# Twenty low-part subtractions move from GpSimd to VectorE, and all units get a new order

## The chip, the cores and the metric

The kernel runs on one core of a Trainium2 chip. The metric is the device time of one execution in microseconds, and less is better. TensorE (PE) multiplies, VectorE (DVE) and ScalarE (ACT) do elementwise work, GpSimd (POOL) does a little of it and issues some transfers, and SyncE (SP) issues the other transfers.

## The reference

Pooled attention is followed by a gated feed-forward layer:

```python
k_p = k.reshape(B, H, Sp, 8, D).mean(axis=3)       # B = H = 8, S = 576, D = 64, Sp = 72
v_p = v.reshape(B, H, Sp, 8, D).mean(axis=3)
scores = matmul(q, k_p.T) / sqrt(D)
attn = exp(scores - max); attn = attn / (attn.sum() + 1e-9)
x = matmul(attn, v_p)        # then heads side by side: 4608 tokens x 512
out = (1 / (1 + exp(-(x @ w_gate))) * (x @ w_val)) @ w_out     # 512 -> 1536 -> 512
```

## The kernel before

The 4608 tokens are worked on in nine blocks of 512. Block 0 goes through attention and the whole layer in a first pass (`first_pass`), in which the 64-bit weights also arrive, are turned into float32 (`conv`, `oconv`) and are split into a high and a low part; attention of blocks 1 and 2 lies in that pass too. Blocks 1 to 8 follow in four pairs. Each pair is one multiplication by Strassen's scheme with seven products: first the two products with the weights of gate and value (`product`; its banks in PSUM are the tiles `chain`), then the one with the output weights (`second_sums`; tiles `acc`). Attention of the next blocks is woven between.

Every operand x is a high part (x rounded to the format fp32r, by ACT) and a low part (x minus the high part, by DVE or POOL), and each product takes three matmuls: high by high, high by low, low by high. So a tile such as `hs` (hidden values), `xo` (tokens), `parts` and `oparts` (weights), `ph` and `pl` (attention weights), `vh` and `vl` (values) is made by one ACT copy and one subtraction.

The values: `vsum` adds eight rows, `vhi` (ACT) writes `vh`, `vlo` writes `vl`; `rsum`, `rhi` and `rlo` do the same for the last eight keys of four heads (tile `other` or `vrc`), and `vput` (POOL) places those in `vres`. In blocks 3 to 8 DVE makes every `vl`. In the first pass, for blocks 1 and 2, POOL does (`v_lo`, `r_lo`).

In blocks 5 to 8 the attention weights are not turned by PE. DVE turns them in blocks of 32 (`turned`, tile `turn`), POOL sends each tile to memory in 4, 8 or 12 small transfers, and a further POOL transfer brings it back (`pt`, `pr`). The tile `turn` has one buffer, so the next turning waits until all of those transfers have read it.

The weights' parts are kept in memory (`kept...`) and loaded again for each pair by transfers on SP's queue.

No scheduler decides the order. The code first records every unit (one instruction, or a group that stays together). The string `LATER` is a list of unit numbers, worked out by a planner beforehand, and the units are issued in that order. Each engine runs its own instructions strictly in that order, and so do the queues of SP and POOL; an instruction that waits holds up everything behind it on its engine.

```python
for n in LATER.split() or range(len(book.units)):
    for taken in book.units[int(n)]:
        taken.issue(link)
```

Of the kernel before, what the change touches and what calls it, by code (L numbers as in the profile page):

```python
# [11 lines left out]
F32 = mybir.dt.float32  # L12
# [314 lines left out]
def attention_then_ffn(ctx: ExitStack, tc: tile.TileContext, qT, kT, vm, vr, vn, sums8, wgv, wo, const, out, outT):  # L327
# [800 lines left out]
    def first_pass():  # L1128
# [202 lines left out]
        def v_lo(j, p):  # L1331
            i = slot(j, p)
            if j:
                for r in (slice(0, D), slice(D, P)):
                    nc.gpsimd.tensor_tensor(out=vl[i][r, r], in0=vs[j, p][r], in1=vh[i][r, r].bitcast(F32), op=ALU.subtract)
                return
# [196 lines left out]
```

## Time and profile before

| What | Value |
| --- | --- |
| Median of 3 runs | 926.18 us |
| Lowest and highest of them | 920.35 and 928.2 us |
| The profiled execution's own time | 930.2 us |
| Its span, first to last instruction | 928.1 us |
| Mean granted clock of TensorE | 0.996 |

The profile shows one execution. Its span leaves out 2.1 us of its time. PE, DVE, ACT, POOL are the engines; PEld is the loading of weights into PE; SPq is SP's queue. All of the recorded instructions carry line L314, because a helper issues them, so the rows are told apart by the tiles that they write and read.

### The profile page before, as it was taken

Reading aid. Unit: us, or ns where it says so; the run is one execution under the profiler, and the core shown is the slowest. Engines: PE = TensorE matmul, PEld = TensorE weight load, DVE = VectorE, ACT = ScalarE, POOL = GpSimd, SP = SyncE. Lnnn points to the kernel's source line nnn. Section 1 sums busy time; section 2 is a strip of 40 time slices with the busy share of each in tenths; the row PEclk is TensorE's granted clock in tenths of the full one; section 3 lists DMA queues with packets and bytes.
Section 4 is the critical chain, followed back from the end, with each engine's and each line's share of the span. In section 5 each row is a group of like instructions: output and inputs, shape, how many; then the busy total and the mean of one; then the engine's idle time right before and its main releaser. Section 6 shows DMA issues by size and latency. Waiting matters only on the chain.

```text
span 928.1 us, 12622 instructions
## 1 busy us (share of the span) xinstructions
PE 901.8 (97%) x4188; PEld 739.7 (80%) x4188; DVE 653.0 (70%) x1024; ACT 550.7 (59%) x1136; POOL 170.8 (18%) x328
## 2 busy tenths in 40 slices
PE   6999998999999998999999999999999999999997
PEld 5778777888888876887888888888888788888886
DVE  7988786998888988755668987444579572332863
ACT  7999895888878654643546664535255553224352
POOL 1122202011121004435244204042212100000000
PEclk9999999999999999999999999999999999999999
DMA  9897897698878688786887797767647857465653
GB/s 348 286 333 299 308 331 288 222 354 303 295 253 284 224 270 257 250 300 204 293 282 225 238 323 215 275 215 257 213 145 246 282 176 255 160 207 189 215 182 114
DMA packets 98448, 234.67 MB, mean 253 GB/s; under 512 B 13008, under 2 KB 33872, under 8 KB 96848
## 3 DMA queue, kind: packets, MB, share of 16 engines
q1 hardware_dynamic: 85328, 203.97, 65.4%
q0 software_dynamic: 13056, 29.90, 9.4%
q8 instruction: 33, 0.54, 0.2%
q14 instruction: 31, 0.25, 0.1%
HBM read 174.58 MB, written 59.24 MB: 252 GB/s over the span
## 4 chain that ended last, share of the span: by engine, by line
PE 75%; DMA 7%; DVE 7%; ACT 6%; issue 3%; POOL 2%; SPq 0%; DVEq 0%; ACTq 0%; POOLq 0%
PE chain L314 46%; PE acc L314 22%; PE sc L314 3%; PE av L314 3%; DMA turned<-turn 2%; DMA h<-keptwG 1%; DMA oparts<-keptS 1%; DVE early L314 1%; DMA keptwV<-w 1%; DMA oparts<-keptO 1%; ACT early L314 1%; POOL turned L314 1%; DVE hs L314 1%; DVE w L314 1%; DMA raw<-in_vr 1%
## 5 line engine op out<-in xcount | busy, mean ns | idle before, releaser
L314 PE MATMUL chain<-xo,parts 128*128 128x512 f32 x2316 | 543.8, 392 | 2.4 <-ACT chain L314 0.9
L314 PEld LDWEIGHTS chain<-xo,parts 128*128 128x128 f32 x2316 | 431.4, 188 | 96.2 <-DVE parts L314 2.2
L314 PE MATMUL acc<-hs,oparts 128*128 128x512 f32 x1008 | 238.1, 392 | 5.3 <-DVE hs L314 3.7
L314 PEld LDWEIGHTS acc<-hs,oparts 128*128 128x128 f32 x1008 | 188.2, 188 | 47.3 <-DVE hs L314 4.9
L314 POOL DMA_DIRECT2D turned<-turn x192 | 105.2, 550 | 254.9 <-DVE turn L314 211.0
L314 DVE TENSOR_TENSOR y<-chain,sV 128x512 f32<-128x512 f32 x46 | 31.3, 685 | 80.6 <-PE chain L314 62.7
L314 DVE TENSOR_TENSOR hs<-h,hs 128x1024 fp32r<-128x1024 f32 x52 | 62.9, 1216 | 16.0 <-ACT hs L314 16.0
L314 ACT CAST hs<-h 128x1024 fp32r<-128x1024 f32 x52 | 54.4, 1050 | 25.6 <-PE acc L314 23.2
L314 ACT COPY chain<-chain 128x512 f32<-128x512 f32 x46 | 26.6, 577 | 70.0 <-PE chain L314 66.0
L314 ACT COPY sV<-chain 128x512 f32<-128x512 f32 x46 | 26.7, 584 | 47.8 <-PE chain L314 38.5
L314 ACT CAST hs<-s 128x1024 fp32r<-128x1024 f32 x36 | 37.6, 1051 | 25.3 <-DVE s L314 18.1
L314 ACT ACT_TABLE_LOAD x39 | 50.0, 1283 | 1.5 <-DVE pm L314 0.9
L314 DVE TENSOR_TENSOR hs<-s,hs 128x1024 fp32r<-128x1024 f32 x36 | 43.4, 1217 | 9.0 <-ACT hs L314 8.9
L314 DVE TENSOR_TENSOR y<-chain,sG 128x512 f32<-128x512 f32 x46 | 30.9, 683 | 24.5 <-PE chain L314 11.8
L314 DVE TENSOR_TENSOR h<-chain,gate 128x512 f32<-128x512 f32 x46 | 31.3, 682 | 22.0 <-PE chain L314 18.0
L314 ACT COPY sG<-chain 128x512 f32<-128x512 f32 x46 | 26.8, 589 | 30.2 <-PE chain L314 30.1
L314 ACT ACTIVATE gate<-chain 128x512 f32<-128x512 f32 x46 | 26.9, 597 | 29.0 <-PE chain L314 28.4
L314 PE MATMUL sc<-kbd,raw 128*128 128x144 f32 (+1 forms) x262 | 41.9, 298 | 2.2 <-POOL kbd L314 2.0
L314 PEld LDWEIGHTS sc<-kbd,raw 128*128 128x128 f32 (+1 forms) x262 | 33.4, 176 | 11.5 <-issue 3.4
L314 PE MATMUL acc<-oparts,hs 128*128 128x512 f32 x144 | 40.0, 407 | 0.0
L314 DVE TENSOR_REDUCE m<-sc 128x4 f32<-128x288 f32 x48 | 21.6, 451 | 17.5 <-PE sc L314 17.5
L314 ACT ACTIVATE gate<-y 128x512 f32<-128x512 f32 x46 | 28.5, 631 | 5.6 <-DVE y L314 5.5
(195 smaller groups left out, 1119.3 us busy)
## 6 DMA issues: line engine op xcount, KB each, us to landing
oparts<-keptS SPq DMA_DIRECT2D x48, 512.0 KB, 4.7
oparts<-keptO SPq DMA_DIRECT2D x72, 256.0 KB, 4.4
raw<-in_wgv SPq DMA_DIRECT2D x12, 1024.0 KB, 8.3
out<-o SPq DMA_DIRECT2D x34, 256.0 KB, 4.4
raw<-in_kT SPq DMA_DIRECT2D x28, 288.0 KB, 4.7
raw<-in_qT SPq DMA_DIRECT2D x29, 256.0 KB, 4.9
raw_o<-in_wo SPq DMA_DIRECT2D x12, 512.0 KB, 6.4
raw<-in_vm SPq DMA_DIRECT2D x24, 256.0 KB, 5.2
```

The source lines that it names most:

```text
L314: return self._book.take(lambda: f(*args, **named))
```

## The change

Two subtractions change their engine, and the order of all units is another. The units themselves, their number and what they compute stay as they were. In the first pass 16 instructions that write `vl` (four heads' pairs, two blocks, two halves) and 4 that write the low part of the last keys leave POOL for DVE.

```diff
 LATER = """
-5 4 3 6 10 2 7 13 24 17 20 12 8 27 26 16 18 30 9 0 21 22 34 19 35 36 25 42 49 50 39 38 83 32 31 11 41 43 47 73 29 55
...
-                    nc.gpsimd.tensor_tensor(out=vl[i][r, r], in0=vs[j, p][r], in1=vh[i][r, r].bitcast(F32), op=ALU.subtract)
+                    nc.vector.tensor_tensor(out=vl[i][r, r], in0=vs[j, p][r], in1=vh[i][r, r].bitcast(F32), op=ALU.subtract)
...
-            nc.gpsimd.tensor_tensor(
+            nc.vector.tensor_tensor(
                 out=vrc[j, g][64:96], in0=vsr[j, g][64:96], in1=vrc[j, g][64:96].bitcast(F32), op=ALU.subtract
             )
```

Three places show what the order does. The first is late in the first pass, on the engine that makes `vl4_103`, the low part of a pair of heads of block 2; before, this is POOL:

```order
L314 TENSOR_TENSOR vl1_100<-early_216,vh1_95 64x64 x2
L314 TENSOR_TENSOR vl4_103<-early_216,vh4_98 64x64
L314 TENSOR_TENSOR vl0_99<-early_216,vh0_94 64x64
L314 TENSOR_SCALAR vres4_108<-other_221,cst_84 96x64 x2
L314 TENSOR_SCALAR vres0_104<-other_221,cst_84 96x64
L314 TENSOR_SCALAR vres1_105<-other_221,cst_84 96x64
...
L314 TENSOR_TENSOR vl4_103<-early_216,vh4_98 64x64
L314 TENSOR_TENSOR vl0_99<-early_216,vh0_94 64x64
```

In the change it is DVE, and the rows around it are conversions of weights (`w4`, `parts`, `w_o`):

```order
L314 TENSOR_TENSOR vl4_103<-early_216,vh4_98 64x64
L314 SCALAR_TENSOR_TENSOR w4_392<-w4_392,raw64_380 128x1024
L314 TENSOR_TENSOR early4_217<-tp_393,early4_217 128x512
L314 TENSOR_TENSOR r3_389<-rest_388,r3_389 128x4x32
L314 TENSOR_TENSOR parts_402<-w4_392,parts_402 128x2x256
L314 TENSOR_TENSOR parts_405<-w4_392,parts_405 128x2x256
L314 TENSOR_TENSOR vl4_103<-early_216,vh4_98 64x64
L314 TENSOR_SCALAR w_o_400<-w_o_400 128x1024
```

The second half of `vl4_103` stood behind six placings of `vres` on POOL, and now stands behind five DVE instructions after its first half, among the conversions.

The second place is on PE at the same stage, where the first `acc` matmul needs `oparts_406` from ACT. Before:

```order
L314 MATMUL chain_401<-xo1_266,parts_397 128x512 x6
L314 MATMUL chain_401<-xo2_271,parts_397 128x512 x6
L314 MATMUL chain_398<-xo1_266,parts_395 128x512 x6
L314 MATMUL chain_410<-xo1_266,parts_405 128x512 x6
L314 MATMUL chain_410<-xo2_271,parts_405 128x512 x6
L314 MATMUL chain_398<-xo2_271,parts_395 128x512 x6
L314 MATMUL acc_315<-oparts_406,hs_404 128x512
```

The same place in the change:

```order
L314 MATMUL chain_398<-xo1_266,parts_395 128x512 x6
L314 MATMUL chain_398<-xo2_271,parts_395 128x512 x6
L314 MATMUL chain_401<-xo1_266,parts_397 128x512 x6
L314 MATMUL chain_401<-xo2_271,parts_397 128x512 x6
L314 MATMUL chain_410<-xo1_266,parts_405 128x512 x6
L314 MATMUL chain_407<-xo1_266,parts_402 128x512 x6
L314 MATMUL chain_407<-xo2_271,parts_402 128x512 x6
L314 MATMUL chain_410<-xo2_271,parts_405 128x512 x6
L314 MATMUL acc_313<-oparts_406,hs_404 128x512
```

The twelve matmuls of `chain_407` now stand ahead of the first `acc` matmul; before, they stood behind it.

The third place is on DVE at the end of the first pair, between the turning of the rest (`turn_848`) and the next turning of block 5 (`turn_855`); `hs_809` and `hs_813` are low parts that `acc` matmuls need soon. Before:

```order
L314 STREAM_TRANSPOSE turn_848<-r3_846 128x384
...
L314 TENSOR_TENSOR o_811<-acc_756,sV5_774 128x512
L314 TENSOR_TENSOR hs_809<-h_423,hs_809 128x1024
L314 TENSOR_TENSOR s_783<-s_783,xs0_495 128x1024
L314 STREAM_TRANSPOSE turn_855<-pm_853 128x512
L314 TENSOR_TENSOR pm_866<-e_819,rz_843 128x512
L314 TENSOR_TENSOR hs_813<-h_424,hs_813 128x1024
L314 TENSOR_TENSOR xo6_796<-s_783,xo6_796 128x1024
L314 TENSOR_TENSOR s_783<-xs0_495,s_783 128x1024
```

The same place in the change:

```order
L314 STREAM_TRANSPOSE turn_848<-r3_846 128x384
...
L314 TENSOR_TENSOR xo6_796<-s_783,xo6_796 128x1024
...
L314 TENSOR_TENSOR hs_807<-h_425,hs_807 128x1024
L314 TENSOR_REDUCE ks_883<-raw_884 128x72
L314 TENSOR_TENSOR hs_809<-h_423,hs_809 128x1024
L314 TENSOR_TENSOR hs_813<-h_424,hs_813 128x1024
L314 TENSOR_TENSOR s_783<-xs0_495,s_783 128x1024
L314 STREAM_TRANSPOSE turn_855<-pm_853 128x512
L314 TENSOR_TENSOR vl0_99<-vs_859,vh0_94 64x64
```

`hs_813`, `xo6_796` and the last sum `s_783` stood behind the turning, and now stand ahead of it.

## Rows read from the trace of the kernel before

**Rows 1.** The page's part 1: busy time, share of the span, instructions of each engine.

```profile
PE 901.8 (97%) x4188; PEld 739.7 (80%) x4188; DVE 653.0 (70%) x1024; ACT 550.7 (59%) x1136; POOL 170.8 (18%) x328
```

**Rows 2.** Busy time by stretch: engines in us, granted clock, DMA share, GB/s.

```profile
20.00:140.00 120.00, 115.24 (x559) 91.66 (x559) 103.45 (x164) 114.00 (x263) 21.49 (x40) 1.00 0.90 315
140.00:160.00 20.00, 17.21 (x85) 14.36 (x84) 12.44 (x20) 11.38 (x28) 6.62 (x12) 0.93 0.83 299
360.00:380.00 20.00, 16.31 (x67) 12.70 (x66) 13.41 (x16) 10.63 (x18) 7.84 (x15) 0.91 0.68 215
760.00:860.00 100.00, 100.00 (x443) 82.75 (x442) 29.69 (x46) 32.25 (x56) 0.00 (x0) 1.00 0.62 205
```

**Rows 3.** PE's waits: total us, times, longest; the whole span.

```profile
PE sc L314 <- DMA h<-in_qT: 5.5, 1, 5.5
PE acc L314 <- DVE hs L314: 3.7, 1, 3.7
PE av L314 <- POOL vl L314: 2.8, 1, 2.8
PE sc L314 <- POOL kbd L314: 2.0, 2, 1.6
...
PE acc L314 <- DMA oparts<-keptS: 1.0, 2, 0.7
PE chain L314 <- ACT chain L314: 0.9, 1, 0.9
...
PE chain L314 <- DVE y L314: 0.5, 1, 0.5
```

**Rows 4.** The timeline near 153 us: start, us, engine, operation, idle before.

```profile
152.38 2.50 POOL L314 TENSOR_SCALAR vres<-other,cst 96x64 fp32r<-96x64 f32 x6
...
154.87 2.48 DVE L314 TENSOR_TENSOR xo<-xs,xo 128x1024 fp32r<-128x1024 f32 x2
154.97 2.55 POOL L314 TENSOR_TENSOR vl<-early,vh 64x64 fp32r<-64x64 f32 x2
...
156.32 0.45 PE L314 MATMUL av<-ph,vl 128*128 128x384 f32 x1 [2.79 <-POOL vl L314]
```

**Rows 5.** The timeline from 352 to 371 us.

```profile
352.50 4.91 POOL L314 DMA_DIRECT2D turned<-turn  x9 [55.75 <-DVE turn L314]
...
358.09 1.62 POOL L314 DMA_DIRECT2D turned<-turn  x3 [0.68 <-DMA turned<-turn]
...
365.98 0.71 DVE L314 STREAM_TRANSPOSE turn<-pm 128x512 f32<-128x512 f32 x1 [4.22 <-DMA turned<-turn]
...
367.34 1.22 DVE L314 TENSOR_TENSOR hs<-h,hs 128x1024 fp32r<-128x1024 f32 x1
...
368.61 2.36 PE L314 MATMUL acc<-hs,oparts 128*128 128x512 f32 x5 [3.69 <-DVE hs L314]
```

**Rows 6.** The timeline from 417 to 425 us.

```profile
417.09 0.71 DVE L314 STREAM_TRANSPOSE turn<-pm 128x512 f32<-128x512 f32 x1 [2.76 <-issue]
...
421.65 1.66 PE L314 MATMUL chain<-xo,parts 128*128 128x512 f32 x6 [0.46 <-DVE y L314]
...
424.20 2.13 PE L314 MATMUL chain<-xo,parts 128*128 128x512 f32 x8 [0.89 <-ACT chain L314]
```

**Rows 7.** The tile `vl`: count, ns min/median/max, first and last start.

```profile
L314 DVE TENSOR_TENSOR vl<-vs,vh x40: 152/220/224, 195.2 to 689.4; 64x64 fp32r<-64x64 f32 x40
L314 POOL TENSOR_TENSOR vl<-early,vh x16: 309/342/1307, 62.0 to 156.3; 64x64 fp32r<-64x64 f32 x16
```

**Rows 8.** Groups by form: count, busy us, mean ns, idle before and its releasers.

```profile
L314 POOL TENSOR_TENSOR other<-early,other 32x64 fp32r<-32x64 f32 x4 | 1.3, 315 | 9.0 <-ACT other L314 9.0
L314 DVE STREAM_TRANSPOSE turn<-pm 128x512 f32<-128x512 f32 x16 | 11.3, 706 | 16.0 <-DMA turned<-turn 13.2 <-issue 2.8
```

**Rows 9.** Transfers: count, KB each, median us from issue to landing.

```profile
oparts<-keptS SPq DMA_DIRECT2D x48, 512.0 KB, 4.7
...
parts<-keptG0C SPq DMA_DIRECT2D x3, 512.0 KB, 6.8
```

307 rows, old and new, of the table LATER are left out of this document.

## The prediction

> **What bounds the kernel now.** I read the engines' busy time first. PE is busy 901.8 of 928.1 us, 97% [rows 1]; the other engines are not the bound on average. The change takes no matmul away, so it can only give back time in which PE waits or runs at the lower clock. The idle part is 928.1 − 901.8 = 26.3 us. The mean granted clock of 0.996 costs about 0.004 × 928.1 = 3.7 us more. Together that is 30.0 us, and no order of the same units can win more than that.
>
> The stretches come second, because the mean hides where these 30 us lie. Late in the program, from 760 to 860 us, PE is busy 100.00 of 100.00 us at full clock: 443 matmuls, 226 ns each [rows 2]. Nothing is to be had there. From 20 to 140 us it is busy 115.24 of 120.00, so 4.76 us are lost, and here ACT is busy 114.00 and DVE 103.45 of 120: ACT is the tight engine, DVE has 16.55 us left. Two stretches show a clock under 1: 0.93 from 140 to 160 and 0.91 from 360 to 380, each beside a long idle time of PE.
>
> The waits come third; they name what PE waited for [rows 3]. The longest, 5.5 us for the first transfer, is the start and stays. Then 3.7 us for `hs`, 2.8 us for `vl` from POOL, 2.0 us for `kbd` from POOL, 1.0 us for loads of `oparts`, and small ones for ACT's `chain` (0.9) and DVE's `y` (0.5).
>
> The timelines tell where the two long ones come from. Near 153 us POOL is still at six `vres` until 154.9 us and only then makes two `vl`, in 2.55 us, while DVE runs two 128x1024 subtractions; PE's `av` starts after 2.79 us of idle [rows 4]. Near 353 us the turning of the rest is sent to memory in 12 transfers, which POOL issues from 352.5 to 359.7 us. The next turning on DVE has no other buffer, waits 4.22 us for them and starts at 365.98. The low part `hs` stands behind it and starts at 367.34, and PE gets its operand at 368.61, after 3.69 us [rows 5].
>
> **The change part by part.** The sum is made against the profiled execution's 930.2 us.
>
> *Low parts on DVE.* Sixteen `vl` at DVE's 220 ns instead of POOL's 342 [rows 7], and four of the last keys (32x64; POOL takes 315 ns [rows 8]; no DVE row has this shape, so I take the 220 ns too): 20 × 0.22 = 4.4 us more on DVE. POOL loses at least 16 × 0.342 + 1.3 = 6.8 us. All of it lies before 160 us. If DVE bound PE there, the 4.4 us would come on the path; with 16.55 us of DVE idle and ACT as the tight engine I take them as covered. If that cover is gone, they cost up to 4.4.
>
> The trace shows that two of these on POOL took 2.55 us beside DVE's two-input subtractions, and the slowest 1307 ns against 309 at best [rows 4, 7]. The Trainium skill, "SBUF — State Buffer", section "SBUF: two separate sides", says that DVE and GpSimd share a port pair as an exclusive lock, and the loser is held up entirely; the trace agrees with its 1307 ns. By the rule the move also ends a mutual hold-up of about 1 us a piece at most, which the sum has as part of the 153 us term.
>
> *The order up to 140 us.* Twelve matmuls of `chain_407` now stand ahead of the first `acc` matmul that needs `oparts_406` from ACT. That gives ACT 12 × 0.226 = 2.7 us more to make it. Of the 4.76 us that PE loses in this stretch I take 2.0 back. Bounds: −2.7 (all of the slack counts) and +4.4 (DVE, above).
>
> *The stall at 153 us.* In the change the two halves of `vl4_103` stand five DVE instructions apart, instead of behind six `vres`. The wait of 2.79 us goes, and with it the lower clock that followed: 0.07 × 20 = 1.4 us. That is −4.2. Bounds: −4.2 and 0, since an instruction of the 128x1024 kind in front takes DVE 1.24 us each [rows 4], and PE may wait for that in place of POOL. I take the whole because the order now puts the last half well ahead of the conversions that follow. Next in line there is ACT's `vh`, which stands in front either way.
>
> *The stall at 365 us.* `hs_813`, `xo6_796` and the last `s_783` are moved ahead of the turning. The turning may wait as before without PE noticing; behind it stand only a `vl` of the next block and later work. The 3.69 us go, and 0.09 × 20 = 1.8 us of lower clock: −5.5. Bounds: −5.5 and −1.8 (if `hs` is then late for another reason by half of the time). The transfers that POOL issues for the turned tile land as late as they did; the tile is read much later.
>
> *Near 421 us.* A turning stands at 417.09 and PE idles 0.46 for `y` and 0.89 for ACT's `chain` shortly after [rows 6]. In the whole trace the turnings account for 16.0 us of idle DVE, 13.2 of it for the transfers [rows 8]. Counted in the order, the turnings were as little as 3 us of matmuls apart, and are now at least 9. So I take both waits away: −1.35. Bounds: −1.35 and 0.
>
> *`kbd` and the loads.* POOL is rid of 6.8 us early on; of the 2.0 us for `kbd` I take half, −1.0 (0 to −2.0). Loads of weights can start when the buffer's last reader is done. The order before leaves 36 loads fewer than 24 matmuls (5.4 us) between that reader and the first use; the order after leaves 15. They land after 4.7 us and 6.8 us in the median [rows 9], so 24 matmuls are about the border. The loads of `oparts` cost 1.0 us [rows 3]; I take half, −0.5 (0 to −1.0).
>
> *What gets tighter.* A change that gives transfers more time takes it from something else. I counted, after the first 150 us, the PE instructions whose operand or bank is finished from a matmul only one group of six (1.36 us) earlier: 43 before, 68 after. The rows price 43 of these at 0.9 + 0.5 = 1.4 us, 0.033 each [rows 3]. I double that, because the small waits aren't all shown: 25 × 0.06 = +1.5. Bounds: 0, and 25 × 0.9 = 22 if each costs as much as the worst. And where a stall goes, the next one appears: when PE is no longer held at 153 and 365 us, it comes earlier to every later hand-over. I put +3 for that, a fifth of what is removed; bounds 0 and 7.
>
> Sum: −2.0 − 4.2 − 5.5 − 1.35 − 1.0 − 0.5 = −14.55; with +1.5 and +3: −10.05. The profiled execution would come to 920.1 us.
>
> This execution is 4.0 us over the median, so it has waits that the median execution lacks. The removed 14.55 are about half (0.48) of all that PE loses (30.0), so I take 0.48 × 4.0 = 1.9 of the missing 4.0 to be among them. The median gains 10.05 − 1.9 = 8.1: **918 us**, 0.9% less. A change of about 1% (9.3 us) is what measurements of this kernel can tell from none, and the forecast is just at that line.
>
> **The rivals.** *The turnings still hold DVE.* What is moved ahead of a turning must itself be ready: `hs` needs its hidden values from ACT. If DVE waits there instead, or POOL's 12 issues now delay a later turning with another `hs` behind it, the gains of 5.5 and 1.35 stay out: 918 + 6.85 = 924.9. For it: the tile still has one buffer, and 13.2 us of DVE's idle time before turnings is waiting for transfers [rows 8]. Against it: the distances have grown.
>
> *The windows are too tight.* If the 25 new ones cost 0.4 each, near the 0.5 of `y` and half of the 0.9 of `chain`, that is 10.0 instead of 1.5: 918 + 8.5 = 926.5, no change. It decides from 0.38 each. Against it: the 43 that exist together show only two such waits.
>
> *The first pass gives more.* If ACT, at 114.00 of 120 us, was held up by DVE and POOL through shared buffers, the rest of the 4.76 and of the `kbd` come back as well: 2.8 + 1.0, and the +3 doesn't come: 918 − 6.8 = 911. For it: the new order is worked out for the whole program. Against it: ACT's own work fills the stretch.
>
> *Slower: DVE becomes the bound of the first pass.* Each low part needs ACT's high part directly in front of it. POOL waited 9.0 us on four of them, 2.25 each [rows 8], and could afford it. On DVE the whole queue would stand behind. If each of the 20 holds DVE for as long as one 128x1024 operation, 1.24 us [rows 4], they cost 20 × (1.24 + 0.22) = 29.2 us against 16.55 us of idle: 12.7 over. The first pass then gives none of its 2.0 + 4.2 + 1.0: 918 + 7.2 + 12.7 = 938. It decides from 16.55 / 20 − 0.22 = 0.61 us lost on each. Against it: the planner's order puts other DVE work between two of them, as the piece with `vl4_103` shows. The Trainium skill, "Perfetto Trace Analysis", section "Optimizing Scalar/DVE Operations", speaks for this case: where DVE is full, work may be taken off it, even to GpSimd, which is the opposite of this change. With DVE at 103.45 of 120 us [rows 2] the trace doesn't show it full, so the chance stays small.
>
> **How the numbers follow.** The forecast's case has 0.50; it spans 912 to 923 by its bounds for the terms 153 us, 421 us, `kbd` and what comes next, with a bit under half of it below 916.9, the 1% line. The turnings 0.18, the tight windows 0.13, the better first pass 0.11, the slower case 0.08. Faster by over 1%: 0.23 + 0.11, and 0.04 of the turnings' case, should its other terms reach their better ends: 0.38. Slower by over 1% (above 935.4): 0.08, and 0.01 of the tight windows at their upper bound: 0.09. The rest, 0.53, is within 1%. The range reaches from 909, just under the better first pass, to 929, over the tight windows with 3 us for their spread; it leaves out the slower case and the outer ends of the others, under 0.2.
>
> **What would show it.** Right: no `av` wait for `vl` and no clock below 1 from 140 to 160; `hs` not among PE's waits; the clock near 1 from 360 to 380; DVE's busy time up by about 4.4 us and POOL's down by 7 or more; PE busy as before, with about 16 us of idle. Wrong: many new short waits of `chain` and `acc` for ACT and DVE of 0.4 us or so (tight windows); a turning that waits with `hs` behind it (turnings); DVE waiting for `vh` on `vl`, and PE busy far less than 115 of 120 us in the stretch up to 140 (slower). The prediction would be most wrong if a transfer that was covered now lands late once per pair: four times a wait like 3.7 us with the lower clock behind it is 22 us, and no row of before shows whether one is near.

## The result and the profile after

The change runs in 916.17 us (median of 7 runs, 913.89 to 918.23), the kernel before in 928.2 us (7 runs, 920.35 to 931.01). The ratio is 0.9882, with a 95% interval of 0.9849 to 0.9915: 1.2% faster. The means, 926.99 and 916.08 us, give that ratio and a gain of 10.9 us; the medians differ by 12.0. The forecast was 918.

The engines' busy time of the profiled execution (its span is 914.4 us) answers to [rows 1]:

```profile
PE 899.3 (98%) x4188; PEld 736.4 (81%) x4188; DVE 657.6 (72%) x1044; ACT 551.5 (60%) x1136; POOL 161.8 (18%) x308
```

PE does the same 4188 matmuls. Its idle time is 914.4 − 899.3 = 15.1 us instead of 26.3, so 11.2 of the 13.7 us that the span lost are idle time of PE. The mean granted clock rose from 0.996 to 0.998, which is worth 3.7 − 1.8 = 1.9 us of the rest. DVE has 20 instructions and 4.6 us more, POOL 20 and 9.0 us fewer.

The same stretches as in [rows 2] (columns as there):

```profile
20.00:140.00 120.00, 117.43 (x569) 93.41 (x567) 106.04 (x182) 111.48 (x261) 17.27 (x28) 0.99 0.88 315
140.00:160.00 20.00, 20.00 (x107) 16.87 (x106) 17.36 (x29) 15.39 (x36) 1.72 (x4) 1.00 0.84 296
360.00:380.00 20.00, 20.00 (x93) 15.57 (x93) 14.67 (x25) 10.82 (x17) 11.99 (x22) 1.00 0.89 301
760.00:860.00 100.00, 100.00 (x442) 82.42 (x441) 38.04 (x51) 34.07 (x56) 0.00 (x0) 1.00 0.60 200
```

In both stretches that had a lower clock, PE is now busy all of the time, and the clock is 1.00. For PE the stretch from 760 to 860 us is as it was. A lower clock stands in another place now, early in the first pass:

```profile
20.00:40.00 20.00, 19.76 (x94) 14.61 (x92) 19.75 (x35) 19.70 (x29) 1.55 (x4) 0.91 0.89 321
```

PE's waits, as in [rows 3]:

```profile
PE sc L314 <- ACT kbd L314: 5.1, 1, 5.1
PE av L314 <- ACT y L314: 1.5, 1, 1.5
PE tp L314 <- ACT vh L314: 1.2, 1, 1.2
PE chain L314 <- ACT chain L314: 0.6, 2, 0.4
```

The first is the start. The waits for `hs`, for `vl`, for `kbd` from POOL and for loads of `oparts` are all gone. The next two lie in the first pass, the two for `chain` at 224 and 250 us. The wait of 1.5 us is at 126 us, where ScalarE had been held up by a transfer of input weights (columns of the timeline: start, us, engine, operation, idle before):

```profile
121.43 1.12 ACT L314 ACTIVATE w<-raw 128x1024 f32<-128x1024 f32 x1 [2.11 <-DMA raw<-in_wgv]
```

The wider stretches tell where the small waits went. Before:

```profile
140.00:320.00 180.00, 176.84 (x850) 145.86 (x849) 151.53 (x275) 141.11 (x354) 28.23 (x52) 0.99 0.79 277
400.00:600.00 200.00, 198.20 (x920) 163.51 (x919) 143.06 (x227) 105.89 (x188) 66.45 (x121) 1.00 0.79 259
```

After:

```profile
140.00:320.00 180.00, 179.31 (x875) 147.89 (x874) 158.79 (x287) 144.26 (x356) 23.31 (x44) 1.00 0.82 287
400.00:600.00 200.00, 199.79 (x928) 164.29 (x927) 142.37 (x225) 103.18 (x186) 59.41 (x108) 1.00 0.80 262
```

From 400 to 600 us PE's idle time fell from 1.80 to 0.21 us. From 140 to 320 us it fell from 3.16, of which 2.79 were the stall for `vl`, to 0.69.

Near the place of [rows 5] the timeline of the change reads:

```profile
345.34 0.57 DVE L314 STREAM_TRANSPOSE turn<-r 128x384 f32<-128x384 f32 x1
...
360.04 0.70 DVE L314 STREAM_TRANSPOSE turn<-pm 128x512 f32<-128x512 f32 x1
...
372.05 0.71 DVE L314 STREAM_TRANSPOSE turn<-pm 128x512 f32<-128x512 f32 x1 [0.92 <-DMA turned<-turn]
```

The second turning, which waited 4.22 us before, starts without a wait. The group of all these turnings answers to the second row of [rows 8]; its idle time is 3.0 us instead of 16.0:

```profile
L314 DVE STREAM_TRANSPOSE turn<-pm 128x512 f32<-128x512 f32 x16 | 11.3, 703 | 3.0 <-DMA turned<-turn 3.0
```

### The profile page after: what moved, and what is told of

Same layout as the page of the kernel before. It is cut to its first block, busy times and chain, and to the rows that moved or that the text cites. A ratio compares the mean times of both kernels' runs of the same rounds, so it can differ in the third digit from the quotient of the medians.

```text
span 914.4 us, 12636 instructions
## 1 busy us (share of the span) xinstructions
PE 899.3 (98%) x4188; PEld 736.4 (81%) x4188; DVE 657.6 (72%) x1044; ACT 551.5 (60%) x1136; POOL 161.8 (18%) x308
## 2 busy tenths in 40 slices
DMA packets 98448, 234.67 MB, mean 257 GB/s; under 512 B 13008, under 2 KB 33872, under 8 KB 96848
## 4 chain that ended last, share of the span: by engine, by line
PE 87%; ACT 5%; DVE 3%; DMA 3%; issue 1%; SPq 1%; ACTq 0%; DVEq 0%
PE chain L314 51%; PE acc L314 28%; PE sc L314 4%; PE av L314 3%; DVE early L314 1%; DMA raw<-in_wgv 1%; ACT e L314 1%; DMA w<-keptWO 1%; DMA keptS<-sums 1%; PE tp L314 1%; ACT L314 1%; DMA h<-in_qT 1%; SPq L314 1%; DVE parts L314 0%; ACT parts L314 0%
## 5 line engine op out<-in xcount | busy, mean ns | idle before, releaser
L314 PE MATMUL chain<-xo,parts 128*128 128x512 f32 x2316 | 545.5, 392 | 0.9 <-ACT chain L314 0.6
L314 PEld LDWEIGHTS chain<-xo,parts 128*128 128x128 f32 x2316 | 429.4, 188 | 96.8 <-DVE parts L314 2.0
L314 PE MATMUL acc<-hs,oparts 128*128 128x512 f32 x1008 | 236.9, 391 | 0.2 <-issue 0.2
L314 PEld LDWEIGHTS acc<-hs,oparts 128*128 128x128 f32 x1008 | 188.0, 188 | 41.1 <-DVE hs L314 1.2
L314 POOL DMA_DIRECT2D turned<-turn x192 | 105.3, 551 | 244.1 <-DVE turn L314 220.5
L314 ACT CAST hs<-h 128x1024 fp32r<-128x1024 f32 x52 | 54.6, 1050 | 43.7 <-PE acc L314 30.2
L314 DVE TENSOR_TENSOR y<-chain,sV 128x512 f32<-128x512 f32 x46 | 31.3, 684 | 56.9 <-PE chain L314 53.5
L314 DVE TENSOR_TENSOR hs<-h,hs 128x1024 fp32r<-128x1024 f32 x52 | 63.1, 1218 | 10.4 <-ACT hs L314 10.1
L314 ACT COPY chain<-chain 128x512 f32<-128x512 f32 x46 | 26.6, 578 | 51.3 <-PE chain L314 47.1
L314 DVE TENSOR_TENSOR y<-chain,sG 128x512 f32<-128x512 f32 x46 | 31.1, 685 | 34.7 <-PE chain L314 29.7
L314 ACT COPY sG<-chain 128x512 f32<-128x512 f32 x46 | 26.6, 587 | 48.4 <-PE chain L314 48.3
L314 ACT CAST hs<-s 128x1024 fp32r<-128x1024 f32 x36 | 37.7, 1052 | 23.6 <-DVE s L314 14.9
L314 DVE TENSOR_TENSOR hs<-s,hs 128x1024 fp32r<-128x1024 f32 x36 | 43.6, 1218 | 10.7 <-ACT hs L314 10.4
L314 DVE TENSOR_TENSOR h<-chain,gate 128x512 f32<-128x512 f32 x46 | 31.3, 683 | 22.9 <-PE chain L314 21.9
L314 ACT ACTIVATE gate<-y 128x512 f32<-128x512 f32 x46 | 28.5, 630 | 28.7 <-DVE y L314 28.6
L314 ACT COPY sV<-chain 128x512 f32<-128x512 f32 x46 | 26.5, 586 | 26.3 <-PE chain L314 26.3
L314 PE MATMUL sc<-kbd,raw 128*128 128x144 f32 (+1 forms) x262 | 41.1, 297 | 0.4 <-DVE e L314 0.4
L314 PEld LDWEIGHTS sc<-kbd,raw 128*128 128x128 f32 (+1 forms) x262 | 32.5, 176 | 9.5 <-issue 4.0
L314 DVE TENSOR_REDUCE m<-sc 128x4 f32<-128x288 f32 x48 | 21.7, 453 | 22.0 <-PE sc L314 21.9
L314 PE MATMUL acc<-oparts,hs 128*128 128x512 f32 x144 | 37.4, 398 | 0.0
L314 ACT ACTIVATE gate<-chain 128x512 f32<-128x512 f32 x46 | 26.8, 595 | 10.7 <-PE chain L314 8.9
```

Source lines behind the costliest of these rows:

```text
L314: return self._book.take(lambda: f(*args, **named))
```

## The experiments

Each kernel was timed against the kernel before on the same chip. The first four below stand beside 926.55 us; both turnings later, the first of the two on the first pass and the two with extra transfers beside 927.42; the others beside 927.33. The helper's line is L308 or L333 in some of these kernels, in place of L314.

**The engine alone.** The order of before, with the twenty low parts on VectorE:

```diff
-                    nc.gpsimd.tensor_tensor(out=vl[i][r, r], in0=vs[j, p][r], in1=vh[i][r, r].bitcast(F32), op=ALU.subtract)
+                    nc.vector.tensor_tensor(out=vl[i][r, r], in0=vs[j, p][r], in1=vh[i][r, r].bitcast(F32), op=ALU.subtract)
...
-            nc.gpsimd.tensor_tensor(
+            nc.vector.tensor_tensor(
```

> The order of before, with only the twenty low parts moved to VectorE. Theory (each part has its own share): the wait of 2.8 us for the low part near 153 us and the lower clock behind it go, and some of the waits for kbd, so about 4 to 5 us less than before, near 923.5 on the scale where before is 928; the wait of 3.7 us near 365 us stays. Rival (the order carries everything, and the engine alone brings nothing, since DVE's queue makes the low parts as late as GpSimd did): within 1.5 us of before, or up to 4 us slower if DVE waits for ScalarE's high parts in front of each.

Measured: 923.64 us, ratio 0.9967 (0.9942 to 0.9991). The stretch around 153 us and the wait near 365 us in its trace:

```profile
140.00:160.00 20.00, 20.00 (x107) 16.98 (x106) 16.19 (x32) 11.86 (x29) 3.94 (x4) 1.00 0.84 304
```

```profile
PE acc L314 <- DVE hs L314: 3.2, 1, 3.2
```

The stall for `vl` and the lower clock are gone, the wait for `hs` is still there. It gives about 3 us, 0.8 to 5.4 by its interval.

**The order alone.** The change, with the two lines above turned round.

> The order of the change, with only the twenty low parts back on GpSimd. Theory (each part has its own share): a stall for a low part returns in the first 160 us, so 3 to 5 us more than the change, near 920. Rival (the order carries everything): the same as the change within 1 us, near 916. A third: the order was made for low parts on DVE, and on GpSimd they hold more than one place: 924 or more.

Measured: 917.93 us, ratio 0.9894 (0.9856 to 0.9932). Its interval and that of the change overlap nearly whole. The same stretch, and the tile `vl` (count, shortest, median and longest in ns):

```profile
140.00:160.00 20.00, 20.00 (x107) 16.91 (x106) 16.85 (x24) 15.40 (x37) 3.22 (x8) 1.00 0.85 298
```

```profile
L314 POOL TENSOR_TENSOR vl<-early,vh x16: 313/354/1410, 58.5 to 149.4; 64x64 fp32r<-64x64 f32 x16
```

Here too PE is busy throughout, with the low parts on GpSimd. So either half of the change removes the stall at 153 us. In the new order nothing that can be measured is left for the engine. The slowest `vl` on GpSimd still took 1410 ns against 313 at best, at 80.6 us, beside a DVE operation on two operands of 1.21 us; PE didn't wait for it. The Trainium skill, "SBUF — State Buffer", section "SBUF: two separate sides", says that the two engines share a port pair, which, when DVE's operation has two inputs in SBUF, one of them holds for its whole instruction while the other is blocked. The spread agrees with it, and it cost nothing here.

**Three instructions ahead of the turning.** The kernel before, with three units moved in the table (1909 is `turn_855`, 1832 `hs_813`, 1793 `xo6_796`, 1845 the last `s_783`):

```diff
-... 1831 1834 1791 1792 1909 1835 2076 1672 1942 1837 1912 1832 1836 1911 1929 1917 1793 1916 1839 1913 1845 ...
+... 1831 1834 1791 1792 1832 1793 1845 1909 1835 2076 1672 1942 1837 1912 1836 1911 1929 1917 1916 1839 1913 ...
```

> The kernel before, with three DVE instructions (the low parts hs_813 and xo6_796 and the last sum s_783) moved ahead of the turning turn_855. Theory: the 3.7 us and the lower clock behind them go: 5 to 5.5 us less than before, near 923, PE's wait for hs is not among its waits. Rival (the three wait for ScalarE in front of the turning, and the turning then delays what follows): less than 2 us gained.

Measured: 925.37 us, ratio 0.9981 (0.996 to 1.0002). The wait for `hs` is gone. But the next turning on DVE now waits, and PE behind it (timeline):

```profile
365.98 0.70 DVE L308 STREAM_TRANSPOSE turn<-pm 128x512 f32<-128x512 f32 x1
...
379.19 0.71 DVE L308 STREAM_TRANSPOSE turn<-pm 128x512 f32<-128x512 f32 x1 [4.52 <-DMA turned<-turn]
...
380.53 1.64 PE L308 MATMUL chain<-xo,parts 128*128 128x512 f32 x6 [2.02 <-DVE y L308]
```

From 360 to 400 us PE loses as much as before, 1.49 + 2.17 = 3.66 us of idle time in place of 3.69, though at full clock:

```profile
360.00:380.00 20.00, 18.51 (x84) 14.59 (x82) 14.27 (x18) 12.33 (x20) 7.34 (x14) 1.00 0.84 267
380.00:400.00 20.00, 17.83 (x84) 14.29 (x85) 14.81 (x30) 9.96 (x22) 6.94 (x13) 1.00 0.86 280
```

The wait of 4.2 us was passed on, 13 us later, as one of 4.5. That the three instructions' place alone gives the 5.5 us does not stand.

**The turning back ahead, in the change.** Unit 1909 is placed in front of 1832 again:

```diff
-... 1835 1980 1832 2076 1829 1877 1845 1836 1994 1827 1909 1839 ...
+... 1835 1980 1909 1832 2076 1829 1877 1845 1836 1994 1827 1839 ...
```

> The kernel after the change, with the turning turn_855 moved back ahead of hs_813. Theory (the place of the turning is the cause): a wait for hs of 2 to 4 us returns near 355 us, 3 to 5 us more than the change, near 920. Rival (it is the earlier turning of the rest, which stands at 345.3 us instead of 351.5, so that its transfers have landed): under 1 us more, near 916.

Measured: 916.57 us, ratio 0.9878 (0.984 to 0.9915), the same as the change. The turnings in its trace:

```profile
344.79 0.57 DVE L308 STREAM_TRANSPOSE turn<-r 128x384 f32<-128x384 f32 x1
...
357.03 0.70 DVE L308 STREAM_TRANSPOSE turn<-pm 128x512 f32<-128x512 f32 x1
```

It starts 12.24 us after the first one without waiting. In the kernel before it could start only 14.46 us after it (351.52 to 365.98 in [rows 5] and the row below). In this order the place of the turning costs nothing, because its buffer is free. The DMA engines' share (second column from the end) speaks for the reason. In the kernel before, the transfers of the first turning fly here:

```profile
350.00:355.00 5.00, 5.00 (x30) 4.37 (x29) 4.89 (x8) 2.65 (x4) 2.49 (x5) 1.00 0.89 279
355.00:360.00 5.00, 5.00 (x23) 4.09 (x22) 5.00 (x7) 1.76 (x4) 4.03 (x8) 1.00 0.87 239
360.00:365.00 5.00, 4.92 (x22) 3.75 (x20) 1.76 (x2) 3.46 (x6) 0.00 (x0) 1.00 0.91 277
```

```profile
351.52 0.58 DVE L314 STREAM_TRANSPOSE turn<-r 128x384 f32<-128x384 f32 x1
```

In the change they fly here:

```profile
345.00:350.00 5.00, 5.00 (x23) 4.14 (x23) 4.29 (x5) 0.68 (x1) 3.69 (x7) 1.00 0.82 281
350.00:355.00 5.00, 5.00 (x25) 4.22 (x25) 4.60 (x6) 2.71 (x6) 2.85 (x6) 1.00 0.75 230
355.00:360.00 5.00, 4.99 (x23) 3.75 (x22) 3.68 (x4) 2.97 (x6) 0.00 (x0) 1.00 0.30 61
```

In the change SP's queue issues three loads of `oparts` among them and then nothing until 357.58 us; in the kernel before it issues ten transfers from 352.69 to 362.80. The DMA engines' traffic in the change from 344 to 374 us, in 40 slices of 0.75 us, is 0 from 355.25 to 358.25:

```profile
346.36 5.56 SPq L314 DMA_DIRECT2D oparts<-keptS  x3
357.58 0.32 SPq L314 DMA_DIRECT2D w<-keptwG  x1
```

```profile
GB/s 342 406 83 360 336 194 410 224 191 355 237 124 300 285 43 0 0 0 0 109 202 262 382 393 372 366 406 250 220 318 335 374 183 109 191 408 187 251 306 363
```

So the turning's transfers were done by 355.25, at most 9.9 us after it started, instead of 14.46. That SP's transfers are what delayed them in the kernel before is read from the rows; no run took them alone away. In the change itself the second turning also comes later, 14.70 us after the first (345.34 to 360.04), so it would have been free of transfers as slow as before, too; the distance alone was not tried.

**Both turnings later.** As three instructions ahead, with the next turning (1943, `turn_868`) and its four transfers that stood among them moved behind unit 1995, past the two sums `y`:

```diff
-... 2077 1967 2080 1943 1922 1985 2001 1970 1968 1947 1940 1953 2006 1951 2078 1960 1948 2002 1995 1993 ...
+... 2077 1967 2080 1922 1985 2001 1970 1968 1940 2006 2078 1960 2002 1995 1943 1947 1953 1951 1948 1993 ...
```

> The kernel before, with three DVE instructions ahead of turn_855 as in the earlier run, and also the next turning, turn_868, moved behind five DVE instructions (two of them the sums y that PE waited 2.0 us for). Theory (what counts is the time from one turning to the next, since the transfers of one need 12 to 14 us, and the wait moved on to the next turning in the earlier run): no wait of PE near 365 nor near 380 us, 3.5 to 5.5 us less than before, near 922.5 where before is 927. Rival (the wait is only pushed on again, to the third turning or to a load): not better than the earlier run, 1 to 2 us less than before.

Measured: 928.17 us, the median of nine executions, ratio 1.0007 (0.9985 to 1.0029). The tenth, the profiled one, took 1819 us and isn't read. For a trace the kernel ran again:

> The same kernel as the earlier run with both turnings later, whose profiled execution was disturbed; this is for its trace alone. Theory (the transfers of a turning compete with loads of weights, and a turning placed later only moves the wait): PE has no wait for hs near 365 us, but a new one of 2 us or more behind turn_868 or behind the third turning, or for loads of oparts. Rival (the distance of the turnings is enough): the waits near 365 and 380 us are gone and no new one stands there, and the time lost is in another stretch.

That execution took 928.64 us. Its PE waits near 365 and 380 us are gone, and this one has come (timeline, then the stretch):

```profile
390.15 0.91 PE L308 MATMUL sc<-kbd,raw 128*64 128x144 f32 x6 [3.78 <-DVE e L308]
```

```profile
380.00:400.00 20.00, 16.22 (x73) 13.27 (x72) 10.53 (x22) 8.86 (x17) 7.04 (x13) 0.91 0.79 281
```

Now no turning waits near here. The wait runs through three in-order queues: POOL's load back of the turned tile (`pt`) waits for the same kind of transfers, ACT's `ph` waits for `pt`, and DVE's `y` for the `gate` behind `ph`:

```profile
379.86 0.58 POOL L308 DMA_DIRECT2D pt<-turned  x1 [4.82 <-DMA turned<-turn]
386.67 0.62 ACT L308 CAST ph<-pt 128x512 fp32r<-128x512 f32 x1 [4.49 <-DMA pt<-turned]
387.85 0.69 DVE L308 TENSOR_TENSOR y<-chain,sV 128x512 f32<-128x512 f32 x1 [4.83 <-ACT gate L308]
```

A stall of 3.8 us with a clock of 0.91 stands 22 us later than in the kernel before. Each of the two repairs by hand passed the wait on to a later place of the in-order queues.

**The stretch around the turnings in the new order.** Of the table of before, only places 1700 to 2099 are sorted as the change has these units; low parts on GpSimd:

```python
place = {n: k for k, n in enumerate(new)}
order = old[:1700] + sorted(old[1700:2100], key=place.get) + old[2100:]
```

> The order of before, in which only the 400 units of the stretch from about 316 to 412 us stand in the order that the change gives them; low parts on GpSimd as before. Theory (the stretch as a whole has to be ordered: turning, loads and low parts together): 5 to 7 us less than before, near 921.5 where before is 927. Rival (the seams at both ends, or what comes later, take it back): under 2 us less.

Measured: 933.12 us, ratio 1.0074 (1.0042 to 1.0106), slower than before. Two rows of its stretches:

```profile
320.00:380.00 60.00, 59.97 (x287) 48.71 (x286) 52.18 (x73) 36.80 (x61) 14.61 (x27) 1.00 0.82 265
400.00:420.00 20.00, 13.79 (x55) 10.98 (x54) 9.12 (x18) 5.80 (x15) 7.14 (x14) 0.86 0.72 243
```

Within the stretch the new order does what it does in the change: 59.97 of 60 us busy, full clock. At its end, where the old order goes on, PE stops for 6.21 us:

```profile
416.32 16.19 PE L308 MATMUL chain<-xo,parts 128*128 128x512 f32 x60 [6.21 <-ACT sG L308]
```

**The first pass in the new order.** Twice, both with low parts on VectorE. One takes the order of the change up to the 780th matmul and then all that is left in the order of before; the other sorts places 0 to 1084 of before as the change has them.

```python
order = new[:1073] + [n for n in old if n not in new[:1073]]
order = sorted(old[:1085], key=place.get) + old[1085:]
```

> The order of the change up to the 780th matmul (about 155 us), then all units that are left in the order of before; low parts on VectorE. Theory (gains of the parts add): the first part's share, 5 to 6 us less than before, near 921.5 where before is 927; the wait for hs near 360 us stays. Rival (the engine alone already gives the first part's share): the same as the order of before with the low parts on VectorE, 923.5. A third: the seam costs what the part gives, 926 or more.

Measured: 931.09 us, ratio 1.0036 (1.0012 to 1.006). PE's longest wait, for the high part of weight sums, is at 197 us, 40 us behind the seam:

```profile
PE tp L308 <- ACT sums L308: 6.1, 1, 6.1
```

> The order of before, in which only the first 1085 units (the first pass, up to about 155 us) stand in the order that the change gives them; low parts on VectorE. Theory (parts add): 5 to 6 us less than before, near 921.5 where before is 927, that is 2 us less than moving the low parts alone. Rival (the engine alone gives the share of the first pass, or the seam costs something): 923.5 or more.

Measured: 930.97 us, ratio 1.0044 (1.0021 to 1.0066). PE waits 6.0 us for `parts` from DVE at 197 us. In both, the times say that more is lost behind the seam than the part had given.

**Both stretches.** Places 0 to 1084 and 1700 to 2099 sorted.

> The two reorderings of the other runs together, low parts on VectorE. Theory (two stretches hold nearly the whole gain): 10 to 12 us less than before, near 916, as fast as the change. Rival (the many small waits elsewhere carry a part): 919 to 921.

Measured: 936.42 us, ratio 1.0087 (1.0059 to 1.0116). Both seams stand in its waits:

```profile
PE chain L308 <- ACT sG L308: 6.3, 1, 6.3
PE chain L308 <- DVE parts L308: 6.1, 2, 5.7
```

So "parts of an order add up" failed in all four runs, and how much each stretch of the new order is worth by itself can't be read from times of such mixtures.

**Loads that land later.** The kernel before and the change, each with a further transfer on SP's queue ahead of each of the 264 loads of kept weights. It computes nothing:

```diff
 for n in LATER.split() or range(len(book.units)):
+    if int(n) in LOADS:
+        extra = dram.tile([P, 256], F32, name=f"extra{n}")
+        tc.nc.sync.dma_start(extra, qT[0, 0][:, :256])
     for taken in book.units[int(n)]:
         taken.issue(link)
```

> The kernel before, with a further transfer of 128 KB on SP's queue ahead of each of the 264 loads of kept weights (35 MB more, computing nothing), so that every load lands later. Theory (the order of before has 36 loads whose lead is under 24 matmuls, the change 15): PE waits for loads at more than ten places, 8 to 20 us more than before. Rival (the leads hardly matter, PE waited 1.4 us for loads in all): under 3 us more.

Measured: 943.24 us, ratio 1.0172 (1.0143 to 1.0202), 15.8 us more than before.

> The kernel after the change with the same 264 further transfers of 128 KB. Theory (leads protect): it loses at most half of what the kernel before loses by them, 2 to 8 us more than the change without them, so the gap between the two orders grows from 11 to 16 us or more. Rival (leads hardly matter): both lose the same, and the gap stays 11.

Measured: 935.54 us, ratio 1.0089 (1.0055 to 1.0123). Without the extra transfers the change would stand at 0.9882 × 927.42 = 916.5, so it lost 19.0 us. PE's waits for loads in the two, the kernel before first:

```profile
PE acc L333 <- DMA oparts<-keptO: 4.5, 5, 1.6
PE acc L333 <- DMA oparts<-keptS: 2.7, 3, 1.8
```

```profile
PE acc L333 <- DMA oparts<-keptO: 5.9, 10, 1.3
PE acc L333 <- DMA oparts<-keptS: 3.1, 2, 2.4
```

The order with fewer short leads lost as much as the other within the intervals, and has more waits for `keptO`, not fewer. The theory that the leads protect doesn't stand.

## Why the prediction was right, and where it was not

The sign, the range and the size of the two large terms were right. To what came, over 1% faster, it gave 0.38, and 0.53 to within 1%; the interval of the ratio lies on both sides of that line. The forecast's gain was 8.1 us from 926.18. Measured from there it is 10.0, and 12.0 from the 928.2 of the seven runs. Between the profiled executions, where no median enters, it is 14.1 against 10.05, and most of that difference is one step.

**The stall at 153 us, −4.2.** As forecast: the idle time went from 2.79 to 0, and the clock from 0.93 to 1.00. The reason was half the story. The prediction gave it to the last half of `vl4_103` on DVE; the order alone does it as well, with that work on GpSimd. And the 1.4 us for the clock are what one execution paid: with the order of before in this place, and the same wait of 2.8 us, the trace of the new order around the turnings has a clock of 1.00:

```profile
140.00:160.00 20.00, 17.21 (x92) 14.37 (x91) 12.77 (x20) 11.89 (x29) 6.63 (x12) 1.00 0.83 304
```

**The stall at 365 us, −5.5.** The size was right: 3.69 us idle to none, clock from 0.91 to 1.00. The mechanism was not, so that the size is in part luck. The step said that three instructions were moved ahead of the turning, that it might wait as before behind them, and that its transfers land as late as they did. Moving the three in the old order gave 1.2 us, with an interval that holds no gain, and the wait passed on; putting the turning back in the new order cost nothing measurable. The transfers were done at most 9.9 us after their turning instead of 14.46, and the turnings' waits are 3.0 us in all instead of 16.0.

**Near 421 us and the loads, −1.35 and −0.5.** Both went: PE's waits there and the 1.4 us for `oparts` aren't in the trace of the change. The reasons aren't shown. Two traces with the order of before in this place, three ahead of the turning and the first of the two on the first pass, have no idle time of PE from 420 to 440 us either. And that the count of leads is the reason isn't borne out by the runs with extra transfers.

**Up to 140 us and `kbd`, −2.0 and −1.0.** The step that gave ACT more time for `oparts_406` has no wait to remove. In the trace of before PE goes from the six groups of `chain` to the first `acc` matmul behind them without idle time:

```profile
129.33 8.60 PE L314 MATMUL chain<-xo,parts 128*128 128x512 f32 x36
137.91 3.02 PE L314 MATMUL acc<-oparts,hs 128*128 128x512 f32 x12
```

The 4.76 us there are waits for `kbd` (1.96, so both terms draw on the same idle time), for `pl` and for DVE's `early`. PE's idle time in the stretch went to 2.57, but the clock of 0.91 from 20 to 40 us costs 0.09 × 20 = 1.8, so only 0.4 of the 3.0 came back. In the trace with the turning back ahead, whose first pass has the same order, the clock is 1.00 and the idle time 2.28, so 2.5 came back there:

```profile
20.00:140.00 120.00, 117.72 (x578) 93.69 (x577) 107.52 (x184) 112.25 (x263) 17.25 (x28) 1.00 0.88 316
```

The `kbd` waits are gone, but 1.5 us at 126 us came. Work on DVE rose from 103.45 to 106.04 of 120 us; PE had no wait for `vl`.

**What gets tighter and what comes up next, +1.5 and +3.** This is the step that failed most, by size: of the 4.5 us little came, the 1.5 at 126 us and two small waits for `chain`. After 400 us PE's idle time fell instead. The 25 additional hand-overs that the prediction counted cost nothing that can be seen: waits for `chain` from ACT are 0.6 us after and 0.9 before, those for `y` from DVE are gone. Counting distances in the order priced nothing here. Without these 4.5 us the sum for the profiled execution would be −14.55; it came from 930.2 to 916.1, −14.1. That it is so near is in part luck: up to 140 us 0.4 came of 3.0, and of the loads' waits 1.4 instead of 0.5.

**The rivals.** The turnings don't hold PE. The windows aren't too tight. The first pass gave less than forecast, not more; that rival also counted the `kbd` waits twice, since they are part of the 4.76. DVE isn't the bound of the first pass: the rival needed 0.61 us lost on each low part, and DVE's busy time rose by 2.6 us in the stretch. The advice named there from "Perfetto Trace Analysis" of the Trainium skill is for a full DVE. From 20 to 40 us DVE is full, 19.75 of 20 us, but the first of the moved low parts runs at 60.1 us.

## What to carry to other kernels

In a program whose engines run in a fixed order, a wait that is repaired at its place can be passed on to a later in-order neighbour: here 4.2 us on DVE became 4.5 us 13 us later, and after a second repair 3.8 us on PE at 390 us. Most of the gain came from an order worked out as a whole, and pieces of it set into the old one were slower than either. When one edit and a new order arrive together, run each alone: here both removed the same stall, and the edit had nothing measurable left to do. Before a term says that more time is given to an operand, look for the wait that it would remove.

## What was not expected of the hardware

Twelve small transfers from one tile held it for 14.46 us beside a DMA share of 0.87 to 0.91, and for at most 9.9 us in the new order, where the share falls from 0.82 to 0.30. Half of the time is their issue on GpSimd: from 352.50 to 359.71, 7.2 us [rows 5].

The same wait of 2.8 us for `vl`, with PE busy 17.21 of 20 us each time, stands beside a granted clock of 0.93, 0.95, 0.90, 0.98 and 1.00 from 140 to 160 us in five traces: the kernel before, three ahead of the turning, both turnings later, extra transfers before, and the new order around the turnings. What the lower clock behind a wait costs can't be read from one execution.

A further 35 MB on 234.67 MB (15% more traffic) cost both orders 1.7 to 2.1%, 15.8 and 19.0 us. In their profiled executions PE's idle time grew by 11.3 and 12.8 us, of which its waits for `oparts` are 5.8 and 9.0, and its busy time for the same matmuls by 5.8 and 5.7; why the busy time grew wasn't taken apart.
